# A long convolution with a gated block: transfers of 100 partitions issued as 96 and 4

## The chip, the cores and the metric

The kernel runs on one core of a Trainium2 chip. The metric is the device time of one execution in microseconds (us). TensorE (PE) multiplies matrices, VectorE (DVE), ScalarE (ACT) and GpSimd (POOL) do elementwise work, and SyncE (SP) issues transfers. ScalarE issues transfers too, in order with its own work. All transfers are moved by the core's 16 DMA engines.

## The reference

The first part is a causal convolution of `u = x * v` with a filter that a small network makes from position embeddings. The second part is a gated block on its result.

```python
h_mlp = np.maximum(pos_emb @ w1, 0.0) @ w2
h_filt = h_mlp * np.exp(-0.01 * pos)[:, None]
u = x * v                                   # (4, 12800, 128)
Uf = np.fft.rfft(u, n=2 * S, axis=1)
Hf = np.fft.rfft(h_filt, n=2 * S, axis=0)
x = x * np.fft.irfft(Uf * Hf[None], n=2 * S, axis=1)[:, :S]
# the gated block
gate_pre = sum(conv_w[k] * xp[:, k:k + S] for k in range(5))   # xp: x with 4 zero rows ahead
out = (sigmoid(gate_pre) * (x @ w_val)) @ w_out
```

Inputs and output are float32, with 4 sequences of 12800 tokens and 128 channels.

## The kernel before

The sequence of 12800 samples is cut in two blocks of 6400, and a block is seen as a grid of `N1` = 100 by `N2` = 64 samples. The transform of a block has two stages: one over the 100 samples of a column, one over the 64 of a row. Where a tile holds the first stage's side, its partitions are the 100 values of `n1` (or of `k1`, or of a row of tokens), so that tile has 100 partitions. Where it holds the second stage's side, its partitions are the 2 x 64 real and imaginary values, so it has 128. Two arrays in DRAM lie between the stages: `a_u`, the spectra after the first stage, and `c_y`, the products after the inverse's first stage.

**Phase 1** (`signal`, `filt`, `fetch`, `prep`) goes over 64 chunks: 2 blocks by 32 pairs of columns. For each chunk `fetch` (L228) has SyncE load 100 partitions of `x` and of `v`, 400 KB each, into a tile of the pool `ld`, which has six buffers. The loads are issued two chunks ahead. `prep` multiplies them on VectorE (`u_t`, L236), rounds the product on ScalarE (`u_hi`, L237) and takes the rest on GpSimd (`u_lo`, L238). Then TensorE does 12 matmuls (`fp`, L264). ScalarE and VectorE evict them into the tile `st` (L267, L269), which has three buffers. Two stores, one issued by ScalarE and one by SyncE (L272), bring 400 KB each to `a_u`. The filter's own steps are dealt out between the chunks: transposes and first matmuls (L174, L182) with eight loads of `pos` (L169), then small matmuls (`ap`, L200 and L201), then the second stage (`fk` L211 and L212, `gz` L214).

**Phase 2** goes over the 100 values of `k1`. It loads `a_u` and a table in tiles of 128 partitions (L351, L346), multiplies, forms the products on VectorE and GpSimd (L311 to L320), transforms back (L326) and stores to `c_y` from a tile of 128 partitions. All its transfers have 128 partitions.

**Phase 3** goes over 8 units (4 sequences by 2 blocks) of 8 chunks. For each chunk `prep` loads `c_y` (L438) and, for every second chunk, `x` (L431, or L434 where the two chunks do not lie together), 800 KB each of 100 partitions, into the same pool `ld`. It rounds on ScalarE (`hi`, L444) and takes the rest on VectorE or GpSimd (`lo`, L447). `conv_out` does the inverse's second stage on TensorE (`y_ps`, L412), times `x` on VectorE (L413), and transposes (L394). The gated block of one unit (`gated_out`) runs beside `conv_out` of the next, its tap sums on VectorE (L462), with output stores of 128 partitions. The first unit has no gated block beside it. The last unit is gated by rows of 100 tokens (`gated_rows`), with output stores of 100 partitions.

The order of the work on each engine is the order in which these generators are advanced in the code. Each issuing engine handles its transfers in that order, and a transfer that waits holds what is queued behind it on its engine.

Three small tables of 100 partitions (`fwd`, `win`, `inv`) are loaded once, at L129, L136 and L137.

Of the kernel before, what the change touches and what calls it, by code (L numbers as in the profile page):

```python
# [16 lines left out]

# The causal convolution of length S = 2 * M is cut in two blocks of M = N1 * N2 samples,
# n = n1 * N2 + n2. A block's polynomial is evaluated at the M roots of z^M = i,
# k = k1 + N1 * k2, in two stages (over n1, then over n2 with the twiddles in the matrix).  # L20
# With z^M = i a product of two real blocks comes back as (low half) + i (high half), so
#   y0 = Re inv(H0 U0),   y1 = Re inv(H0 U1 + (H1 - i H0) U0)
# and no block is padded.
B, S, D, FO, KC = 4, 12800, 128, 64, 5
J, N1, N2 = 2, 100, 64
M = N1 * N2
KG = 8
P1C = 2
CH = 8
# [27 lines left out]
def _narrow(nc, pool, dst, src):  # L57
    """dst (float32) = src, whose 64-bit words are doubles, rounded to nearest."""
    p, n = dst.shape
    raw = pool.tile([p, n], mybir.dt.int64, name="raw")  # L60
    nc.scalar.dma_start(out=raw, in_=src)
    words = raw.bitcast(I32).rearrange("p (n w) -> p n w", w=2)
    lo, hi = words[:, :, 0], words[:, :, 1]
    ve = nc.vector
    top = pool.tile([p, n], I32, name="top")
    tmp = pool.tile([p, n], I32, name="tmp")
    ve.tensor_scalar(out=top, in0=hi, scalar1=0x07FFFFFF, scalar2=3, op0=ALU.bitwise_and, op1=ALU.logical_shift_left)
    ve.tensor_single_scalar(out=tmp, in_=hi, scalar=-0x40000000, op=ALU.bitwise_and)
    ve.tensor_tensor(out=top, in0=top, in1=tmp, op=ALU.bitwise_or)
    ve.tensor_single_scalar(out=tmp, in_=lo, scalar=29, op=ALU.logical_shift_right)  # L70
    ve.tensor_tensor(out=top, in0=top, in1=tmp, op=ALU.bitwise_or)
    # the 29 bits below, in units of the value's own power of two
    ve.tensor_single_scalar(out=tmp, in_=lo, scalar=0x1FFFFFFF, op=ALU.bitwise_and)
    rest = pool.tile([p, n], F32, name="rest")
    ve.tensor_copy(out=rest, in_=tmp)
    ve.tensor_single_scalar(out=tmp, in_=top, scalar=-0x00800000, op=ALU.bitwise_and)
    ve.scalar_tensor_tensor(rest, rest, 2.0 ** -52, tmp.bitcast(F32), op0=ALU.mult, op1=ALU.mult)
    ve.tensor_tensor(out=rest, in0=rest, in1=top.bitcast(F32), op=ALU.add)
    # below float32's range: zero
    ve.tensor_scalar(out=tmp, in0=hi, scalar1=27, scalar2=15, op0=ALU.logical_shift_right, op1=ALU.bitwise_and)  # L80
    keep = pool.tile([p, n], F32, name="keep")
    ve.tensor_single_scalar(out=keep, in_=tmp, scalar=7, op=ALU.is_ge)
    ve.tensor_tensor(out=dst, in0=rest, in1=keep, op=ALU.mult)


@with_exitstack
def tile_longconv_gate(
# [18 lines left out]
):  # L106
    nc = tc.nc
    const = ctx.enter_context(tc.tile_pool(name="const", bufs=1))
    ld = ctx.enter_context(tc.tile_pool(name="ld", bufs=6))
    dram = ctx.enter_context(tc.tile_pool(name="dram", bufs=1, space=DRAM))  # L110

    # spectra after the first stage: [k1][re|im][n2][block][...][d]
    a_u = dram.tile([N1, 2, N2, J, B, D], F32, name="a_u")
    # products after the inverse's first stage: [block][batch][k1][re|im, n2][d]
    c_y = dram.tile([J, B, N1, 2 * N2, D], F32, name="c_y")
# [37 lines left out]

    # the filter's channels before w2, after the first stage: [re|im, n2][k1][block][channel]
    ag_pool = tc.tile_pool(name="ag", bufs=1)
    ag = ag_pool.__enter__().tile([128, N1, J, FO], F32, name="ag")

# [1 line left out]
    with tc.tile_pool(name="p1", bufs=1) as p1, tc.tile_pool(name="ps1", bufs=1, space=PSUM) as ps1:  # L159
# [4 lines left out]
        def filt():  # L164
            HC = 16
            for c0 in range(0, N2, HC):
                pos_sb = load()[:N1].rearrange("a (j n f) -> a j n f", j=J, f=FO)
                for j in range(J):
                    nc.sync.dma_start(out=pos_sb[:, j], in_=pos_v[j][:, c0:c0 + HC])  # L169
                for j in range(J):  # L170
                    for n in range(0, HC, 8):
# [17 lines left out]
                        yield  # L189
            # block 1 holds H1 - i H0  # L190
            E = 4
            for j in range(J):
                for e0 in range(0, FO, E):
# [10 lines left out]
                    yield  # L204
            # the second stage, in place: [block, channel][k1][re|im, k2]
            for k0 in range(0, N1, 4):
# [16 lines left out]
        def fetch(i):  # L223
            j, n0 = chunks[i]
            ns = slice(n0, n0 + P1C)
            t = load()[:N1].rearrange("a (w b e) -> a w b e", w=2, b=B)
            for w, src in enumerate((xv, vv)):
                nc.sync.dma_start(out=t[:, w], in_=src[j][:, :, ns].rearrange("a b n d -> a b (n d)"))  # L228
            return t[:, 0], t[:, 1]
# [15 lines left out]
        def signal():  # L245
            ready = [prep(0)]
            for i, (j, n0) in enumerate(chunks):
# [23 lines left out]
                for c in range(2):  # L271
                    (nc.scalar if c == 0 else nc.sync).dma_start(  # L272
                        out=a_u[:, c, ns, j].rearrange("k n b d -> k n (b d)"),
                        in_=st[:, c].rearrange("k n b d -> k n (b d)"))

        # the filter's steps are spread over the signal's by their time on the tensor engine
        FS = 0.9
# [13 lines left out]

# [1 line left out]
    with tc.tile_pool(name="p2", bufs=1) as p2, tc.tile_pool(name="ps2", bufs=1, space=PSUM) as ps2:  # L293
# [3 lines left out]
        def tail(k1, g_l, z_ps, h_sb):  # L297
# [7 lines left out]

            # [V0 | H0 U1 | H1' U0], then the last two added
            v_t = p2.tile([128, J + 1, BD], F32, name="v_t2", bufs=4)
# [67 lines left out]

# [1 line left out]
    with tc.tile_pool(name="p3", bufs=1) as p3, tc.tile_pool(name="ps3", bufs=1, space=PSUM) as ps3:  # L377
        xv = x.rearrange("b (j a n) d -> b j a n d", j=J, a=N1)
        HALO = KC - 1
# [3 lines left out]
        def conv_out(b, j, ext, rows=None):  # L383
            """y of one block, times x, transposed: ext[d, HALO + token]; with rows, a list
            for the chunks that are done, ext[d, HALO + n2, n1] and the last chunk first"""
            if rows is None:
# [37 lines left out]
        def prep(b, j, q):  # L424
            ns = slice(q * CH, (q + 1) * CH)
            i = order(b, j).index(q)
            if i % 2 == 0:
                x2 = load()[:N1].rearrange("k (n d) -> k n d", d=D)
                two = order(b, j)[i:i + 2]
                if two[1] == two[0] + 1:  # L430
                    nc.sync.dma_start(out=x2, in_=xv[b, j][:, q * CH:(q + 2) * CH])  # L431
                else:
                    for h, qq in enumerate(two):
                        nc.sync.dma_start(out=x2[:, h * CH:(h + 1) * CH], in_=xv[b, j][:, qq * CH:(qq + 1) * CH])  # L434
                x_now[:] = [x2]
            xt = x_now[0][:, i % 2 * CH:(i % 2 + 1) * CH]
            ct = load()[:N1, 0:2 * CH * D].rearrange("k (c e) -> k c e", c=2)
            nc.sync.dma_start(  # L438
                out=ct, in_=c_y[j, b].rearrange("k (c n) d -> k c n d", c=2)[:, :, ns].rearrange("k c n d -> k c (n d)"))
            hi = p3.tile([N1, 2, CH * D], F32R, name="hi", bufs=2)  # L440
            lo = p3.tile([N1, 2, CH * D], F32R, name="lo", bufs=2)
            for h in range(2):
                hs = slice(h * CH * D // 2, (h + 1) * CH * D // 2)
                nc.scalar.copy(out=hi[:, :, hs], in_=ct[:, :, hs])  # L444
                # until the gates run, the vector engine has room for half of this
                eng = nc.vector if h == 0 and (b * J + j) * (N2 // CH) + q < 11 else nc.gpsimd
                eng.tensor_tensor(lo[:, :, hs], ct[:, :, hs], hi[:, :, hs].bitcast(F32), op=ALU.subtract)  # L447
            return hi, lo, xt

        def gate(ext, t0, W=TCH, shift=1, pooled=0):  # L450
            """the gate's elementwise chain, an instruction at a time; pooled: taps added by GpSimd"""
            sl = lambda k: ext[:, t0 + k * shift:t0 + k * shift + W]
# [62 lines left out]
        def gated_rows(b, j, ext, rows):  # L515
            """the same by rows of N1 tokens, each chunk as soon as conv_out has it"""
            W = CH * N1
            for q in order(b, j)[1:] + order(b, j)[:1]:
# [14 lines left out]
                for g0 in range(0, CH, G):  # L533
# [4 lines left out]
                    yield  # L538
                nc.scalar.dma_start(
                    out=out[b, j * M:(j + 1) * M].rearrange("(a n) d -> a n d", a=N1)[:, q * CH:(q + 1) * CH], in_=o_sb)  # L540
# [36 lines left out]

        # the last block goes by rows, so that its gate does not wait for all of it
        b, j = units[-1]
# [49 lines left out]
```

## Time and profile before

| | |
|---|---|
| time, median of 3 runs | 1739.79 us (1730.27 to 1749.66) |
| profiled execution, span | 1744.1 us |
| TensorE / VectorE / ScalarE / GpSimd busy | 77% / 81% / 59% / 67% |
| moved by DMA | 332.97 MB, 191 GB/s in the mean |
| mean granted TensorE clock | 0.887 |

The profiled execution's span lies within the three times, so no separate share around the span can be read off. Phase 1 takes about the first 468 us, phase 2 goes on to about 1103 us, and phase 3 to the end.

A row of the table by stretches has the stretch, its length, and then the busy time and the number of instructions of TensorE, its weight loads, VectorE, ScalarE and GpSimd, followed by the granted clock, the mean busy share of the 16 DMA engines, and GB/s. A row of the chain of waits has a start, a duration and what ran. Rows of waits have who waited at which line, for whom, the total, how often, and the longest. A row of the issues has the tensors, the queue (SPq is SyncE's, ACTq is ScalarE's), the count and the size of one. A row for one line has shortest, median and longest duration in ns, and the first and last start.

### The profile page before, as it was taken

What the parts mean: (1) busy time and instruction counts of PE and PEld (TensorE: products, weight loads), DVE (VectorE), ACT (ScalarE), POOL (GpSimd) and SP (SyncE); (2) the same over time, 40 slices, a digit from 0 to 9 for tenths busy, and PEclk for the clock granted to TensorE, in tenths of its full rate; (3) what the DMA queues carried; (4) which work ended last, traced back from release to release, by engine and by line L of the source; (5) the groups of instructions that cost most, each with busy time, mean ns of one, the idle gap of its engine ahead of it and who ended that gap; (6) DMA issues with size and microseconds to landing.
All of it is one profiled execution on the core that took longest, in us unless ns stands there. A gap on an engine that the chain in (4) does not pass through costs nothing.

```text
span 1744.1 us, 16766 instructions
## 1 busy us (share of the span) xinstructions
PE 1344.8 (77%) x5313; PEld 873.4 (50%) x5313; DVE 1418.7 (81%) x1204; ACT 1032.3 (59%) x1657; POOL 1168.2 (67%) x528
## 2 busy tenths in 40 slices
PE   4679988767677777677777676588888888889896
PEld 3567766544323333233333232356766676667675
DVE  5663337653399999999999999269999999999996
ACT  2235446552477777677777775255656565556765
POOL 2223333333299988878888888159978697788752
PEclk9798997885799989998999999687988998888899
DMA  6666666666656656555656553565555455555512
GB/s 227 243 243 241 246 236 234 241 235 253 220 203 198 212 181 205 179 177 181 203 178 211 173 185 99 170 216 168 183 191 158 159 183 161 172 177 166 177 61 91
DMA packets 224831, 332.97 MB, mean 191 GB/s; under 512 B 7832, under 2 KB 162500, under 8 KB 220108
## 3 DMA queue, kind: packets, MB, share of 16 engines
q1 hardware_dynamic: 99358, 226.12, 38.8%
q10 hardware_dynamic: 125386, 105.79, 18.3%
q8 instruction: 43, 0.70, 0.2%
q14 instruction: 44, 0.36, 0.1%
HBM read 200.80 MB, written 131.07 MB: 190 GB/s over the span
## 4 chain that ended last, share of the span: by engine, by line
DVE 43%; DMA 21%; issue 15%; PE 15%; ACT 3%; POOL 2%; SPq 1%; ACTq 0%; POOLq 0%; DVEq 0%
DVE gt L462 16%; DMA a_u<-st 13%; DVE v_t L316 9%; DVE v_t L317 5%; PE fp L264 4%; DMA ld<-c_y 4%; DVE v_t L311 3%; DVE v_t L312 3%; DMA ld<-in_x_dram 3%; DVE at L413 2%; PE o_ps L506 2%; DVE gd L495 2%; PE y_ps L412 2%; PE z_ps L367 1%; PE c_ps L326 1%
## 5 line engine op out<-in xcount | busy, mean ns | idle before, releaser
L447 POOL TENSOR_TENSOR lo<-ld,hi 100x1024 fp32r<-100x1024 f32 x117 | 373.0, 3209 | 116.9 <-ACT hi L444 115.2
L462 DVE SCALAR_TENSOR_TENSOR gt<-ext,cw,gt 128x1280 f32<-128x1280 f32 (+1 forms) x164 | 411.5, 2521 | 10.2 <-POOL gt L459 5.3
L238 POOL TENSOR_TENSOR u_lo<-u_t,u_hi 100x1024 fp32r<-100x1024 f32 x64 | 154.2, 2411 | 302.3 <-ACT u_hi L237 263.5
L367 PE MATMUL z_ps<-ld 128*128 128x512 f32 x400 | 215.7, 666 | 117.3 <-DVE v_t L312 97.7
L311 POOL TENSOR_TENSOR q_t<-zsw,h_sb 128x1024 f32<-128x1024 f32 x100 | 241.6, 2416 | 90.2 <-ACT zsw L300 90.2
L316 DVE TENSOR_TENSOR v_t<-v_t,q_t 128x1536 f32<-128x1536 f32 x100 | 277.6, 2806 | 1.2 <-POOL q_t L312 1.2
L326 PE MATMUL c_ps<-v_t,ld 128*128 128x512 f32 x400 | 208.0, 639 | 57.2 <-POOL v_t L320 29.1
L312 POOL TENSOR_TENSOR q_t<-zsw,h_sb 128x512 f32<-128x512 f32 x100 | 225.8, 2258 | 0.0
L364 ACT COPY h_sb<-h_ps 64x256 f32<-64x256 f32 x400 | 147.1, 368 | 103.0 <-DVE v_t L312 66.7
L264 PE MATMUL fp<-u_hi,fwd_hi 100*100 100x512 f32 x256 | 127.6, 499 | 90.3 <-ACT st L267 59.3
L269 DVE COPY st<-fp 100x512 f32<-100x512 f32 x128 | 84.6, 687 | 127.9 <-DMA a_u<-st 100.0
L367 PEld LDWEIGHTS z_ps<-ld 128*128 128x128 f32 x400 | 76.6, 206 | 205.8 <-issue 166.9
L506 PEld LDWEIGHTS o_ps<-wout,gd 128*128 128x128 f32 x700 | 167.9, 320 | 11.9 <-issue 2.5
L317 DVE TENSOR_TENSOR v_t<-v_t 128x448 f32<-128x448 f32 x100 | 172.6, 1757 | 0.1
L444 ACT CAST hi<-ld 100x1024 fp32r<-100x1024 f32 x128 | 128.0, 1048 | 71.1 <-DMA ld<-c_y 44.5
L326 PEld LDWEIGHTS c_ps<-v_t,ld 128*128 128x128 f32 x400 | 77.9, 205 | 179.2 <-issue 123.3
L506 PE MATMUL o_ps<-wout,gd 128*128 128x128 f32 x700 | 164.2, 384 | 0.7 <-DVE gd L495 0.7
L299 ACT ACTIVATE zsw<-z_ps 64x1024 f32<-64x1024 f32 x100 | 102.2, 1022 | 61.1 <-PE z_ps L367 56.9
L311 DVE TENSOR_TENSOR v_t<-z_ps,h_sb 128x1024 f32<-128x1024 f32 x100 | 121.1, 1211 | 18.5 <-ACT zsw L300 18.5
L267 ACT COPY st<-fp 100x512 f32<-100x512 f32 x128 | 69.7, 591 | 110.7 <-DMA a_u<-st 85.6
L237 ACT CAST u_hi<-u_t 100x1024 fp32r<-100x1024 f32 x64 | 68.0, 1064 | 107.1 <-PE fp L264 51.6
L236 DVE TENSOR_TENSOR u_t<-ld 100x1024 f32<-100x1024 f32 x64 | 82.5, 1290 | 57.0 <-POOL u_lo L238 49.9
(93 smaller groups left out, 2696.8 us busy)
## 6 DMA issues: line engine op xcount, KB each, us to landing
c_y<-c_sb ACTq DMA_DIRECT2D x100, 512.0 KB
ld<-c_y SPq DMA_DIRECT2D x64, 800.0 KB
ld<-a_u SPq DMA_DIRECT2D x49, 1024.0 KB
ld<-in_x_dram SPq DMA_DIRECT2D x66, 400.0 KB
ld<-in_v_dram SPq DMA_DIRECT2D x64, 400.0 KB
a_u<-st ACTq DMA_DIRECT2D x64, 400.0 KB
a_u<-st SPq DMA_DIRECT2D x64, 400.0 KB
ld<-in_x_dram SPq DMA_DIRECT2D x31, 800.0 KB
```

What stands on the lines that cost most here:

```text
L238: nc.gpsimd.tensor_tensor(lo, u_t, hi.bitcast(F32), op=ALU.subtract)
L264: nc.tensor.matmul(out=fp, lhsT=w[:, c], rhs=d[:, b:b + 2], start=(k == 0), stop=(k == 2))
L311: eng.tensor_tensor(fl(t[:, 0:J]), fl(z), h_b(c, 0, J * B), op=ALU.mult)
L312: eng.tensor_tensor(fl(t[:, J:J + 1]), fl(z[:, 0:1]), h_b(c, 1, B), op=ALU.mult)
L316: nc.vector.tensor_tensor(v_t, v_t, q_t, op=ALU.add)
L317: nc.vector.tensor_tensor(v_t[:, 1, CUT:], v_t[:, 1, CUT:], v_t[:, 2, CUT:], op=ALU.add)
L326: nc.tensor.matmul(out=c_ps, lhsT=g_l, rhs=v_t[:, j], start=True, stop=True)
L364: nc.scalar.copy(out=h_sb[half * N2:(half + 1) * N2, c], in_=h_ps[c * N2:(c + 1) * N2])
L367: nc.tensor.matmul(out=z_ps[:, j], lhsT=f_l, rhs=au[:, j], start=True, stop=True)
L447: eng.tensor_tensor(lo[:, :, hs], ct[:, :, hs], hi[:, :, hs].bitcast(F32), op=ALU.subtract)
L462: nc.vector.scalar_tensor_tensor(gt, sl(k), cw[:, k:k + 1], gt, op0=ALU.mult, op1=ALU.add)
L506: nc.tensor.matmul(out=o_ps[:, i], lhsT=gv[:, g0 + i], rhs=wout, start=True, stop=True)
```

## The change

Every transfer of 100 partitions inside the phases is issued as two: one for partitions 0 to 95 and one for partitions 96 to 99. A small class stands in for the issuing engine and issues both, one after the other, on the same queue. The bytes, the tiles, the buffers, the queues and the order stay the same. The calls concerned are the loads of `pos`, `x` and `v` in phase 1, both stores to `a_u`, the loads of `x` and `c_y` in phase 3, and the output stores of `gated_rows`. The three tables are loaded as before. The rest of the diff removes comments.

```diff
+class _Split:
+    def __init__(self, eng):
+        self.eng = eng
+
+    def dma_start(self, out, in_):
+        for a, b in ((0, 96), (96, N1)):
+            self.eng.dma_start(out=out[a:b], in_=in_[a:b])
...
     nc = tc.nc
+    sync_s, scalar_s = _Split(nc.sync), _Split(nc.scalar)
...
-                    nc.sync.dma_start(out=pos_sb[:, j], in_=pos_v[j][:, c0:c0 + HC])
+                    sync_s.dma_start(out=pos_sb[:, j], in_=pos_v[j][:, c0:c0 + HC])
...
-                nc.sync.dma_start(out=t[:, w], in_=src[j][:, :, ns].rearrange("a b n d -> a b (n d)"))
+                sync_s.dma_start(out=t[:, w], in_=src[j][:, :, ns].rearrange("a b n d -> a b (n d)"))
...
-                    (nc.scalar if c == 0 else nc.sync).dma_start(
+                    (scalar_s if c == 0 else sync_s).dma_start(
                         out=a_u[:, c, ns, j].rearrange("k n b d -> k n (b d)"),
                         in_=st[:, c].rearrange("k n b d -> k n (b d)"))
...
-                    nc.sync.dma_start(out=x2, in_=xv[b, j][:, q * CH:(q + 2) * CH])
+                    sync_s.dma_start(out=x2, in_=xv[b, j][:, q * CH:(q + 2) * CH])
...
-                        nc.sync.dma_start(out=x2[:, h * CH:(h + 1) * CH], in_=xv[b, j][:, qq * CH:(qq + 1) * CH])
+                        sync_s.dma_start(out=x2[:, h * CH:(h + 1) * CH], in_=xv[b, j][:, qq * CH:(qq + 1) * CH])
...
-            nc.sync.dma_start(
+            sync_s.dma_start(
                 out=ct, in_=c_y[j, b].rearrange("k (c n) d -> k c n d", c=2)[:, :, ns].rearrange("k c n d -> k c (n d)"))
...
-                nc.scalar.dma_start(
+                scalar_s.dma_start(
                     out=out[b, j * M:(j + 1) * M].rearrange("(a n) d -> a n d", a=N1)[:, q * CH:(q + 1) * CH], in_=o_sb)
```

## The prediction

> **What bounds the kernel now.** I read the page first, then the busy time of each engine by stretches, then the chain of waits inside the first phase, SyncE's queue beside it, and the list of waits.
>
> ```profile
> span 1744.1 us, 16766 instructions
> PE 1344.8 (77%) x5313; PEld 873.4 (50%) x5313; DVE 1418.7 (81%) x1204; ACT 1032.3 (59%) x1657; POOL 1168.2 (67%) x528
> DMA  6666666666656656555656553565555455555512
> ```
>
> Over the whole span VectorE looks like the bound, at 81%. But the DMA digits stand at 6 through the first eleven slices and never reach 7. The table by stretches shows what that means (PE, PEld, DVE, ACT, POOL busy, clock, DMA share, GB/s):
>
> ```profile
> 0.00:30.00 30.00, 13.31 (x40) 9.01 (x40) 14.30 (x26) 7.74 (x14) 7.26 (x7) 1.00 0.65 217
> 30.00:110.00 80.00, 53.64 (x267) 40.94 (x268) 52.72 (x84) 20.72 (x31) 23.89 (x10) 0.83 0.67 244
> 110.00:190.00 80.00, 75.99 (x587) 58.76 (x585) 33.78 (x50) 39.18 (x54) 26.71 (x11) 0.91 0.67 242
> 190.00:270.00 80.00, 74.32 (x511) 54.96 (x507) 32.16 (x42) 36.80 (x57) 29.08 (x12) 0.94 0.67 240
> 270.00:350.00 80.00, 60.21 (x268) 45.37 (x266) 54.48 (x100) 50.14 (x114) 26.31 (x12) 0.83 0.67 238
> 350.00:430.00 80.00, 57.46 (x191) 38.40 (x192) 36.99 (x56) 33.19 (x62) 28.48 (x12) 0.73 0.68 244
> 430.00:468.00 38.00, 24.08 (x78) 15.12 (x77) 14.95 (x17) 12.86 (x19) 12.69 (x5) 0.72 0.57 192
> 602.50:605.00 2.50, 2.50 (x8) 1.32 (x7) 2.50 (x2) 1.91 (x2) 2.50 (x2) 1.00 0.96 377
> 630.50:635.50 5.00, 4.63 (x13) 2.09 (x11) 5.00 (x2) 4.88 (x10) 4.66 (x2) 1.00 0.97 360
> 1121.00:1165.00 44.00, 34.80 (x150) 22.71 (x149) 18.25 (x22) 21.26 (x30) 17.02 (x8) 0.85 0.62 222
> 1165.00:1187.00 22.00, 18.64 (x68) 12.09 (x67) 22.00 (x16) 13.20 (x20) 21.56 (x7) 0.68 0.59 187
> 1187.00:1650.00 463.00, 398.33 (x1784) 319.48 (x1784) 444.77 (x318) 277.88 (x378) 383.42 (x129) 0.89 0.54 173
> ```
>
> From 30 to 430 us the DMA share is 0.67 or 0.68 in every row, whatever the compute engines do. In phase 2, where all transfers have 128 partitions, short stretches reach 0.96 and 0.97, at 360 to 377 GB/s. So 0.67 is a ceiling of the phase 1 transfers, which have 100 partitions. 0.67 of 16 engines is 10.7. The largest number of engines up to 16 over which 100 rows can be dealt evenly is 10 (128 rows: 16). I read it so: ten engines work without a pause, six stand idle.
>
> The chain of waits and SyncE's queue agree:
>
> ```profile
> 206.05 11.86 DMA a_u<-st
> 219.75 12.22 DMA a_u<-st
> 233.37 12.84 DMA a_u<-st
> ```
>
> ```profile
> 206.05 3.28 SPq L272 DMA_DIRECT2D a_u<-st  x1
> 209.43 0.81 SPq L228 DMA_DIRECT2D ld<-in_x_dram  x1
> 210.30 2.48 SPq L228 DMA_DIRECT2D ld<-in_v_dram  x1
> 212.87 3.30 SPq L272 DMA_DIRECT2D a_u<-st  x1
> ```
>
> ```profile
> DVE st L269 <- DMA a_u<-st: 100.0, 32, 6.2
> ACT st L267 <- DMA a_u<-st: 85.6, 30, 9.5
> SPq L228 <- DMA fwd<-in_tab_fwd_dram: 1.8, 1, 1.8
> ACT hi L444 <- DMA ld<-c_y: 44.5, 13, 12.0
> ```
>
> Nearly the whole chain from 191 to 262 us is stores of `st`: each takes 12 us to land, and the evictions that want its buffer wait (100.0 and 85.6 us). SyncE goes from one issue to the next without a rest, at 2.5 to 3.3 us each: it is held back by full queues. One chunk takes 212.87 - 206.05 = 6.82 us.
>
> From 1187 us on VectorE is 444.77 of 463 us busy: there DMA does not decide. Between them lies phase 3's first block (1103 to 1187 us): VectorE is free (18.25 of 44 us), the share again 0.62, and ScalarE waits for `c_y` (44.5 us).
>
> **The change part by part.** Transfers that become two, by the list of issues:
>
> ```profile
> ld<-c_y SPq DMA_DIRECT2D x64, 800.0 KB
> ld<-in_x_dram SPq DMA_DIRECT2D x66, 400.0 KB
> ld<-in_v_dram SPq DMA_DIRECT2D x64, 400.0 KB
> a_u<-st ACTq DMA_DIRECT2D x64, 400.0 KB
> a_u<-st SPq DMA_DIRECT2D x64, 400.0 KB
> ld<-in_x_dram SPq DMA_DIRECT2D x31, 800.0 KB
> ld<-in_pos_emb_dram SPq DMA_DIRECT2D x8, 400.0 KB
> out_dram<-o_sb ACTq DMA_DIRECT2D x8, 400.0 KB
> c_y<-c_sb ACTq DMA_DIRECT2D x100, 512.0 KB
> ```
>
> The last row, of 128 partitions, stays whole. The others add 64+66+64+64+64+31+8+8 = 369 issues: 297 on SyncE, 72 on ScalarE. The three table loads of 100 partitions stay as they are.
>
> *The rate.* 96 rows deal evenly over 16 engines, six each; the other 4 rows give at best one more to four of them. The busiest engine then moves 7 rows of 100 in place of 10: a factor of 0.70, or 242 / 0.70 = 346 GB/s, below the 360 that phase 2 reaches. The trace has no transfer of 96 or of 4 rows, so this has bounds: 0.63 (100/16 rows, and four engines not felt) to 1.00 (all 4 rows on one engine, 6+4 = 10). I take 0.70, because 128 rows, the nearest row of the kind, do fill 16 engines.
>
> [...]
>
> *Phase 1's loop.* With DMA at 0.70, 80 us become at least 56 and the last 38 become 27. The next bound is TensorE. Its busy column (76.0 and 74.3 of 80 us from 110 to 270) counts modelled ends and stretches at half clock and is an upper bound; weight loads, one per matmul, give the lower one (58.8 and 55.0). I take the middle, 67 and 65. The other stretches have nothing above 60.2 (VectorE at most 54.5, ScalarE 50.1). Floors: 56 + 67 + 65 + 56 + 56 + 27 = 327 us for 438. All engines then stand near their limits together, in queues kept in program order, so I add 9%, an estimate: VectorE as the bound runs at 96% (444.77/463) where one engine decides, and here three do. That makes 357 us, 5.6 us a chunk: gain 81 us. Bounds: 438 - 327 = 111 at best, with the lower TensorE bound 438 - (56+59+56+56+56+27) = 128; at worst below nothing (the rivals).
>
> *Phase 1's head* (30 us): the same kind of transfers at 0.65, but more issues ahead of the tables on which ScalarE waits. I put it at nothing, give or take 5.
>
> *Phase 2*: all its transfers have 128 partitions. Nothing changes.
>
> *Phase 3's first block*: 84 us, held by DMA for the first 62 (1103 to 1165) and by both for 22. At 0.70 the 62 would lose 19; TensorE's 34.80 of 44 us leave at most 9 in the row that is shown, so some 13 of 62. In the 22 VectorE is busy throughout, so I count 2. Gain 15; bounds 5 to 25. After 1187 us VectorE is the bound: nothing.
>
> *The issues themselves.* Held back by nothing, one issue takes:
>
> ```profile
> L272 ACTq DMA_DIRECT2D a_u<-st x64: 281/282/333, 29.8 to 459.1; - x64
> L438 SPq DMA_DIRECT2D ld<-c_y x64: 750/757/897, 1102.7 to 1643.6; - x64
> 1099.39 3.21 DMA c_y<-c_sb
> ```
>
> SyncE issues three transfers per chunk of phase 1, then six: 6 x 0.28 = 1.7 us of 5.6, hidden by the wait for room. ScalarE gets 64 x 0.28 = 18 us more in phase 1, where its busiest stretch is 50.14 of 80. In phase 3, 64 x 0.76 more on SyncE lie ahead of loads two chunks early. A second wait at each reader is hidden with them; uncovered, all 72 on ScalarE would cost 20 us.
>
> *What gets scarcer.* SyncE's fifth load starts only here:
>
> ```profile
> 4.82 0.80 SPq L228 DMA_DIRECT2D ld<-in_x_dram  x1
> ```
>
> It waited for the landing of `fwd`, an unrelated table and the first DMA of the program (1.8 us, in the waits above). Ahead of it stand four loads of SyncE and, in the order of the code and at the same pace, four of ScalarE. I read it as eight completion counters dealt out in turn. A phase 1 chunk has four transfers, so the counters span two chunks; with eight they span one. A transfer must then have landed before its successor one chunk later is issued, with the rest of SyncE's queue, or of ScalarE's evictions, behind it. Landing is 12 us now, but mostly queueing: two chunks are 3.28 MB, 13.5 us at 242 GB/s. One chunk is 1.64 MB, 4.7 us at 346 GB/s. The fixed part, from the 3.21 us of a 512 KB store that has the engines to itself, is 3.21 - 0.524/0.36 = 1.75 us. While one transfer's end is reported, the others keep the engines busy, so I count this within the 9%.
>
> Sum: 1744 - 81 - 15 = 1648 us. The three times, 1730 to 1750 with median 1740, straddle the span, so I take the page's own time as typical.
>
> **The rivals.** *The counters cost the fixed part every time*: a chunk takes 4.7 + 1.75 = 6.5 us against 6.82. Over 63 periods that is 20 us, and 1744 - 20 - 15 = 1709. For it: SyncE issues in order. Against: four transfers in flight cover one another. Chance 0.12.
>
> *Slower*: landing shrinks only with the rate and not with the backlog, 11.86 x 0.70 = 8.3 us; with one chunk per round of counters the period is 8.3, (8.3 - 6.82) x 63 = 93 us more, 1744 + 93 - 15 = 1822. It decides as soon as a landing takes more than 6.8 us. Against it: half the bytes can be waiting. Chance 0.06.
>
> *It does not do what it says*: the pieces do not spread, one engine still moves 10 rows, and the time stays near 1744. For it: no row of this trace has 96 or 4. Against: 128 rows do spread. Chance 0.07.
>
> [...]
>
> **How the numbers follow.** The forecast has 0.75: its own range is 1744 - 128 - 25 = 1591 to about 1690 (loop gain 45, phase 3's 9). The range for 8 in 10 leaves out the bottom of that, where no engine loses anything, and takes in the first rival: 1605 to 1712. Three runs of before spread by 1.1%, so about 1% can be told from no change. Faster by over 1% holds the forecast and most of the first rival, 0.86; within 1%, the third and a rest of the first, 0.08; slower 0.06.
>
> **What would show it.** DMA share above 0.67 in the first slices, toward 0.8 to 0.95, at 290 GB/s or more; phase 1 ending near 387 us in place of 468; waits of L269 and L267 for `a_u<-st` well below 100.0 and 85.6 us; the `a_u<-st` landings at 4 to 6 us; phase 2 as long as before, and VectorE still over 95% busy after the first block. Wrong, if the share stays at 0.67 (no spread), or rises while SyncE's issues wait for landings of older loads (counters), or if TensorE is full from 110 to 270 us and the gain is lost there.

## The result and the profile after

The changed kernel takes 1665.82 us (median, 1663.25 to 1668.40), and the kernel before, beside it on the same chip, 1744.72 us (1730.27 to 1751.33). The ratio is 0.9557, with a 95% interval of 0.9499 to 0.9615. The forecast was 1648 us, with a range of 1605 to 1712. The direction is right and the time lies within the range, but the gain is 79 us where 96 were forecast, and a part of those 79 has a cause that the prediction did not have.

The page of the changed kernel, its span, busy times and DMA digits:

```profile
span 1665.5 us, 17379 instructions
PE 1312.5 (79%) x5313; PEld 855.8 (51%) x5313; DVE 1403.6 (84%) x1204; ACT 1029.6 (62%) x1657; POOL 1184.0 (71%) x528
DMA  9998899997666555665556555786676666676413
```

The first nine slices, which were all 6, are now 8 and 9: by this share, engines that stood idle now work. In phase 2 the line looks as it did, and in phase 3 its digits rise from 5 to 6 and 7.

To see where the 78.6 us between the two spans (1744.1 and 1665.5) come from, I cut both at three points: the first load of `a_u` (phase 1 over), the first product `at` (phase 3 has begun) and the first tap sum `gt` (its first block is over). Each row has the first start behind the three durations. First the kernel before, then the changed one:

```profile
L351 SPq DMA_DIRECT2D ld<-a_u x51: 343/360/484, 468.3 to 1031.2; - x51
L413 DVE TENSOR_TENSOR at<-y_ps,ld x128: 673/678/693, 1118.7 to 1684.5; 100x512 f32<-100x512 f32 x128
L462 DVE SCALAR_TENSOR_TENSOR gt<-ext,cw,gt x164: 1037/2466/6090, 1168.2 to 1733.2; 128x1280 f32<-128x1280 f32 x140, 128x800 f32<-128x800 f32 x24
```

```profile
L363 SPq DMA_DIRECT2D ld<-a_u x51: 344/360/476, 408.0 to 970.9; - x51
L425 DVE TENSOR_TENSOR at<-y_ps,ld x128: 672/678/693, 1060.8 to 1609.7; 100x512 f32<-100x512 f32 x128
L474 DVE SCALAR_TENSOR_TENSOR gt<-ext,cw,gt x164: 1037/2450/6039, 1104.1 to 1654.3; 128x1280 f32<-128x1280 f32 x140, 128x800 f32<-128x800 f32 x24
```

| stage | before | after | gain |
|---|---|---|---|
| phase 1 | 468.3 | 408.0 | 60.3 |
| phase 2, to the first `at` | 650.4 | 652.8 | -2.4 |
| phase 3, first block | 49.5 | 43.3 | 6.2 |
| phase 3, the rest (to the span's end) | 575.9 | 561.4 | 14.5 |

Each column is one execution. A second profile of the changed kernel, from another chip, ends phase 1 at 414.8 us, with 651.6, 42.0 and 563.1 us for the other stages. So some 7 us of phase 1 and 2 of the others can't be told from scatter. Of the kernel before there is one profile, and its executions spread over 21 us, so the gains of single stages rest on the other runs below as well.

The table by stretches of the changed kernel, with the same columns as before:

```profile
30.00:110.00 80.00, 61.16 (x297) 44.52 (x296) 59.10 (x97) 24.12 (x35) 28.90 (x12) 0.89 1.00 297
110.00:190.00 80.00, 78.06 (x657) 62.79 (x656) 30.86 (x36) 40.38 (x54) 26.71 (x11) 0.91 0.87 247
190.00:270.00 80.00, 75.92 (x486) 55.37 (x484) 45.18 (x64) 48.57 (x84) 34.26 (x14) 0.96 0.91 270
270.00:350.00 80.00, 65.65 (x308) 48.43 (x307) 63.57 (x113) 55.77 (x125) 37.64 (x14) 0.89 0.97 292
350.00:400.00 50.00, 38.85 (x139) 24.45 (x140) 27.30 (x32) 22.57 (x35) 27.14 (x11) 0.90 0.90 278
1061.00:1101.00 40.00, 32.98 (x157) 23.62 (x156) 20.62 (x24) 20.86 (x31) 19.77 (x8) 0.84 0.96 220
1123.00:1575.00 452.00, 401.10 (x1826) 324.41 (x1825) 430.34 (x326) 282.52 (x387) 396.49 (x131) 0.91 0.65 178
```

The share is 1.00 from 30 to 110 us and 0.97 from 270 to 350, so the transfers do spread over all 16 engines and still decide there. But full engines move 297 and 292 GB/s, not 346. From 110 to 270 us TensorE is busy 78.06 and 75.92 of 80, and the share falls: there it seems to have taken over. The chain of waits agrees. From 190 to 270 us its steps on TensorE make up about 69% and its transfers 21%, where before the stores of `st` alone made up 92%. From 110 to 190 us the difference is small, 62% on TensorE against 55% before. In phase 3's first block (the row from 1061 us), where only loads run, the share rises from 0.62 to 0.96 but the rate stays, at 220 GB/s against 222. In the last row, after the first block, VectorE is busy 95% of the time, as the prediction said.

The waits of the changed kernel, first those of the engines, then those of SyncE's queue (its line is that of the helper):

```profile
ACT st L279 <- DMA a_u<-st: 7.3, 3, 3.9
DVE st L281 <- DMA a_u<-st: 5.0, 2, 3.3
ACT hi L456 <- DMA ld<-c_y: 29.6, 5, 17.1
...
SPq L94 <- DMA ld<-in_x_dram: 52.3, 50, 2.6
SPq L94 <- DMA ld<-in_v_dram: 45.8, 46, 3.9
SPq L94 <- DMA a_u<-st: 35.6, 50, 1.7
```

The evictions hardly wait for stores any more (85.6 and 100.0 us before). SyncE now does wait for older transfers to land, 134 us in all, though never longer than 3.9 us at a time.

Two places of the chain of waits: stores in phase 1, and phase 2's last store.

```profile
71.93 4.73 DMA a_u<-st
76.74 6.24 DMA a_u<-st
83.06 4.69 DMA a_u<-st
...
1037.99 13.20 DMA c_y<-c_sb
```

A store of `st` lands after 5 to 6 us in place of 12. But phase 2's last store, a transfer that the change doesn't touch, takes 13.20 us where it took 3.21. The head of phase 3 has become slower.

### The profile page after: what moved, and what is told of

Read it like the earlier page. It is cut to its first block, busy times and chain, and to the rows that moved or that the text cites. A ratio compares the mean times of both kernels' runs of the same rounds, so it can differ in the third digit from the quotient of the medians.

```text
span 1665.5 us, 17379 instructions
## 1 busy us (share of the span) xinstructions
PE 1312.5 (79%) x5313; PEld 855.8 (51%) x5313; DVE 1403.6 (84%) x1204; ACT 1029.6 (62%) x1657; POOL 1184.0 (71%) x528
## 4 chain that ended last, share of the span: by engine, by line
DVE 41%; PE 23%; DMA 16%; issue 16%; ACT 2%; POOL 2%; ACTq 0%; SPq 0%; DVEq 0%; POOLq 0%
DVE gt L474 13%; DVE v_t L328 10%; DMA a_u<-st 6%; DVE v_t L329 5%; PE fp L276 5%; PE y_ps L424 4%; DMA ld<-in_v_dram 4%; DVE v_t L323 3%; DVE v_t L324 3%; PE o_ps L518 3%; DVE at L425 2%; PE z_ps L379 2%; DMA ld<-c_y 2%; DVE gd L507 2%; PE c_ps L338 2%
## 5 line engine op out<-in xcount | busy, mean ns | idle before, releaser
L459 POOL TENSOR_TENSOR lo<-ld,hi 100x1024 fp32r<-100x1024 f32 x117 | 379.4, 3269 | 90.3 <-ACT hi L456 86.0
L474 DVE SCALAR_TENSOR_TENSOR gt<-ext,cw,gt 128x1280 f32<-128x1280 f32 (+1 forms) x164 | 386.1, 2369 | 7.4 <-POOL gt L471 7.0
L250 POOL TENSOR_TENSOR u_lo<-u_t,u_hi 100x1024 fp32r<-100x1024 f32 x64 | 163.5, 2559 | 235.4 <-ACT u_hi L249 214.6
L379 PE MATMUL z_ps<-ld 128*128 128x512 f32 x400 | 219.1, 675 | 117.0 <-DVE v_t L324 97.2
L276 PE MATMUL fp<-u_hi,fwd_hi 100*100 100x512 f32 x256 | 117.6, 459 | 53.4 <-ACT u_hi L249 23.7
L248 DVE TENSOR_TENSOR u_t<-ld 100x1024 f32<-100x1024 f32 x64 | 88.5, 1384 | 51.1 <-POOL u_lo L250 34.1
L408 ACT COPY ext<-tp 128x400 f32<-128x400 f32 x128 | 68.4, 542 | 84.3 <-PE tp L406 83.7
L339 ACT COPY c_sb<-c_ps 128x512 f32<-128x512 f32 x200 | 110.8, 588 | 14.2 <-PE c_ps L338 10.7
```

Of the source, the lines that this page charges most:

```text
L250: nc.gpsimd.tensor_tensor(lo, u_t, hi.bitcast(F32), op=ALU.subtract)
L276: nc.tensor.matmul(out=fp, lhsT=w[:, c], rhs=d[:, b:b + 2], start=(k == 0), stop=(k == 2))
L379: nc.tensor.matmul(out=z_ps[:, j], lhsT=f_l, rhs=au[:, j], start=True, stop=True)
L474: nc.vector.scalar_tensor_tensor(gt, sl(k), cw[:, k:k + 1], gt, op0=ALU.mult, op1=ALU.add)
```

## The experiments

All have the kernel before run beside them on their own chip. Below, phase 1 ends at the first load of `a_u`, and "the rest of phase 3" is the span from the first `gt` on.

**Only phase 1's transfers cut.** The four calls of phase 3 go back to whole transfers.

```diff
-            sync_s.dma_start(
+            nc.sync.dma_start(
                 out=ct, in_=c_y[j, b]...   # the same for both loads of x, and for the store of gated_rows
```

> Only the transfers of phase 1 are split. Theory: the gain comes from the rate of each stage's own transfers, so phase 1 ends near 408 us as in the changed kernel (468 before) and phase 3 takes as long as before (about 641 us from its first load of c_y): 1745 - 60 = about 1685 us. Rival: phase 3's later units became shorter (448 to 434 us between the same two chunks) because VectorE and GpSimd happen to meet differently after a changed start, whatever the loads do; then phase 3 shortens here too and the time is 1665 to 1672 us.

Measured: 1665.63 us, ratio 0.9546 (0.9515 to 0.9576). That is the changed kernel's time, and the rival's, so the cuts in phase 3 earn nothing in sum that shows. Its three first starts:

```profile
L363 SPq DMA_DIRECT2D ld<-a_u x51: 344/360/480, 409.8 to 972.8; - x51
L425 DVE TENSOR_TENSOR at<-y_ps,ld x128: 673/678/693, 1057.9 to 1613.0; 100x512 f32<-100x512 f32 x128
L474 DVE SCALAR_TENSOR_TENSOR gt<-ext,cw,gt x164: 1035/2452/6036, 1107.3 to 1655.1; 128x1280 f32<-128x1280 f32 x140, 128x800 f32<-128x800 f32 x24
```

Its first block takes 49.4 us, as before. Yet the rest of phase 3 takes 1665.1 - 1107.3 = 557.8 us, in place of 575.9, although its code is now that of the kernel before.

**Only phase 3's transfers cut.** The three calls of phase 1 go back.

```diff
-                sync_s.dma_start(out=t[:, w], in_=src[j]...)
+                nc.sync.dma_start(out=t[:, w], in_=src[j]...)   # the same for pos and for both stores to a_u
```

> Only the transfers of phase 3 are split. Theory: phase 1 as before (468 us), phase 3 as in the changed kernel, so 1745 - 20 = about 1725 us, with the early 96-row loads of c_y again in the way of phase 2's last stores (first rounding some 17 us after the last of these is issued, 12 before). Rival (a shift of VectorE against GpSimd and not the loads): about 1740 us or more.

Measured: 1728.36 us, ratio 0.9899 (0.9868 to 0.9929). Phase 1 ends at 474.4 us, 6 us later than before, which is no more than the two profiles of the changed kernel differ by. The first block takes 43.5 us, 6 less than before, and the rest of phase 3 takes 558.2 us, as in the run above. So the first block's 6 us belong to phase 3's cuts. The 15 us after it come with either half of the change.

**Twice the transfers, all of 100 partitions.** Each transfer is cut in two by columns.

```diff
-        for a, b in ((0, 96), (96, N1)):
-            self.eng.dma_start(out=out[a:b], in_=in_[a:b])
+        h = out.shape[1] // 2
+        for a, b in ((0, h), (h, 2 * h)):
+            self.eng.dma_start(out=out[:, a:b], in_=in_[:, a:b])
```

> Every transfer that the change splits is split in the free dimension in place of the partitions: two transfers of 100 partitions and half the columns. The number of transfers, and with it the number of issues and of completion counters per chunk, is that of the changed kernel; the rows stay on as many engines as before. Theory (the gain is the spread over more engines, the counters cost next to nothing): phase 1 as before, 468 us give or take 8, and 1735 to 1755 us in all. Rival (the counters cost the fixed part of a landing): a chunk takes 1.64 MB / 242 GB/s + 1.75 us = 8.5 us in place of 6.8, phase 1 is up to 107 us longer, and the time is 1780 to 1850 us. Rival (the gain came from smaller pieces): as fast as the changed kernel, 1666 us.

Measured: 1727.64 us, ratio 0.9900 (0.9875 to 0.9924). The stretch that DMA holds, the first load of `a_u`, and two stores of the chain:

```profile
30.00:110.00 80.00, 54.49 (x248) 39.48 (x246) 47.82 (x84) 19.56 (x29) 23.34 (x10) 0.83 0.67 245
```

```profile
L364 SPq DMA_DIRECT2D ld<-a_u x51: 348/360/605, 468.4 to 1032.1; - x51
```

```profile
34.15 6.76 DMA a_u<-st
...
216.37 6.99 DMA a_u<-st
```

With eight transfers per chunk phase 1 ends at 468.4 us, as before. The number of transfers costs nothing that shows, and cutting alone gives nothing there: share and rate stay at 0.67 and 245 GB/s. The 1% comes after phase 1: 3 us up to the first `at`, 5 in the first block, and 10 in the rest of phase 3 (565.7 us). A store of half the size now lands in 7 us, not 12, at the same rate. Its 200 KB fewer are 0.8 us at 245 GB/s, so by this estimate most of the landing time was backlog.

**Pure movement.** A kernel that leaves out the whole computation and, in one stretch after the other, moves 12 transfers with rows of 8 KB. Each stretch changes one thing: the number of rows, the partition that they start at, or their distance in DRAM.

```python
def load_64_at0(i):
    nc.sync.dma_start(out=big[0:64, i], in_=rows_of(i, 64, 1))
def load_64_at32(i):
    nc.sync.dma_start(out=big[32:96, i], in_=rows_of(i, 64, 1))
def load_96_4_step(i):                      # rows 64 KB apart in DRAM
    s = rows_of(i, 100, 8)
    nc.sync.dma_start(out=big[0:96, i], in_=s[0:96])
    nc.sync.dma_start(out=big[96:100, i], in_=s[96:100])
```

> Leaves out the whole computation and only moves data: seventeen stretches of twelve transfers each, rows of 8 KB. What is asked: why the changed kernel moves 297 GB/s in phase 1 and 220 GB/s in phase 3's first block with all engines busy (share 1.00 and 0.96), where loads of 128 partitions in phase 2 reach 360. [...] Theory D (DRAM: rows that lie 64 KB apart are slow): with rows that lie together 96 and 64 rows anywhere go at over 320 GB/s, and stepped rows at 250 or less with 128 partitions too. [...]

The stretches (start and end, length, busy VectorE and GpSimd, clock, DMA share, GB/s). Loads: 64 rows from partition 0, 64 from partition 32, then rows 64 KB apart: 128, 96, 100, and 96+4. Stores: 128, 100, 96+4.

```profile
255.00:283.00 28.00, 0.00 (x0) 0.00 (x0) 1.00 1.01 206
288.00:303.00 15.00, 0.00 (x0) 0.00 (x0) 1.00 1.01 397
349.00:377.00 28.00, 0.00 (x0) 0.00 (x0) 1.00 1.01 424
381.00:418.00 37.00, 0.00 (x0) 0.00 (x0) 1.00 1.01 248
422.00:470.00 48.00, 0.00 (x0) 0.00 (x0) 1.00 0.57 203
475.00:518.00 43.00, 0.00 (x0) 0.00 (x0) 1.00 0.97 217
572.00:601.00 29.00, 0.00 (x0) 0.00 (x0) 1.00 1.01 420
605.00:646.00 41.00, 0.00 (x0) 0.00 (x0) 1.00 0.61 229
650.00:686.00 36.00, 0.00 (x0) 0.00 (x0) 1.00 0.85 263
```

The same 64 rows move at 206 GB/s from partition 0 and at 397 from partition 32, with all engines busy in both. So the rate depends on which partitions are touched, not only on how many engines work. 96 rows from partition 0 fill the engines (1.01) and move at 248 GB/s (246 from partition 32), where 128 rows reach 424. The distance in DRAM is not the cause, since 128 rows have it too. Loads alone gain little from 96+4 (203 to 217), stores alone somewhat more (229 to 263).

Why 96 rows fall to 248 isn't settled here. The runs show rates by partition; the paths into the on-chip memory that the rivals of two later runs name were not shown.

**Pure movement, other cuts, both directions at once.** The whole computation is left out here too; SyncE loads and ScalarE stores together.

```python
CUTS = {"100": ((0, 100),), "96_4": ((0, 96), (96, 100)), "36_64": ((0, 36), (36, 100)), "128": ((0, 128),), ...}
def load(i, cuts):
    for a, b in cuts:
        nc.sync.dma_start(out=big[a:b, i], in_=s[a:b])
def store(i, cuts):
    for a, b in cuts:
        nc.scalar.dma_start(out=orow[i * 128 + a:i * 128 + b], in_=one[a:b, i % 6])
```

> Leaves out the whole computation and only moves data: twenty stretches of twelve transfers of rows of 8 KB. Asked: what the pieces of four rows cost, and whether other cuts of 100 rows are faster. [...] Stores of 64 rows at 0 against 32 show whether reading the on-chip memory has the same limit: half the rate, or the same.

Both directions with 100, 96+4, 36+64 and 128 rows:

```profile
565.00:642.00 77.00, 0.00 (x0) 0.00 (x0) 1.00 0.62 252
647.00:702.00 55.00, 0.00 (x0) 0.00 (x0) 1.00 0.98 348
767.00:820.00 53.00, 0.00 (x0) 0.00 (x0) 1.00 0.94 362
890.00:947.00 57.00, 0.00 (x0) 0.00 (x0) 1.00 1.01 418
```

With both directions at once 96+4 gains what the prediction counted: 252 / 348 = 0.72. So the factor of 0.70 is about right for mixed traffic in rows of 8 KB, and the cut 0 to 35 and 36 to 99 is better still, at 362. Stores alone agree (262 GB/s with 96+4, 277 with 36+64). Loads alone do not: 96+4 moves 232 GB/s, 36+64 only 219 and 80+20 only 212, so other cuts gain nothing there. Pieces of 4 rows alone move 30 GB/s in loads and 25 in stores, at a share of 0.28 and 0.25. Stores of 64 rows go at 205 GB/s from partition 0 and 416 from partition 32, the same difference that loads have (206 and 397).

**Phase 1, loads alone cut.** As the first run, and both stores to `a_u` whole.

```diff
-                    (scalar_s if c == 0 else sync_s).dma_start(
+                    (nc.scalar if c == 0 else nc.sync).dma_start(
                         out=a_u[:, c, ns, j]...
```

> Only the loads of phase 1 (pos, x, v) are split, its stores are whole again, and phase 3 is whole. Theory (seven rows in place of ten on the busiest engine, for loads and stores alike): 17 rows in place of 20 for a load and a store, a factor of 0.85, phase 1 near 435 us, and with the 18 us of phase 3 that every variant has had: about 1694 us. Rival (paths into the on-chip memory, on which 96+4 rows load at 212 GB/s and 100 rows at 196 in the kernel that only moves data): 0.96, phase 1 near 455 us, 1714 us.

Measured: 1690.49 us, ratio 0.9667 (0.9628 to 0.9707).

**Phase 1, stores alone cut.** As the first run, and the loads of `pos`, `x` and `v` whole.

```diff
-                sync_s.dma_start(out=t[:, w], in_=src[j]...)
+                nc.sync.dma_start(out=t[:, w], in_=src[j]...)   # the same for pos
```

> Only the stores of phase 1 (a_u) are split, its loads are whole again, and phase 3 is whole. Theory (rows on the busiest engine): as for the loads, phase 1 near 435 us, about 1694 us. Rival (paths; stores of 96+4 rows went at 257 GB/s and of 100 at 222): 0.93, phase 1 near 440 us, 1699 us. If the stores' landing as such decides, since the evictions wait for it, this one brings most of the 60 us and the loads little.

Measured: 1696.04 us, ratio 0.9699 (0.9654 to 0.9744). First the run with loads cut, then two first starts of the run with stores cut:

```profile
L363 SPq DMA_DIRECT2D ld<-a_u x51: 349/360/572, 435.1 to 996.5; - x51
```

```profile
L363 SPq DMA_DIRECT2D ld<-a_u x51: 344/360/506, 420.0 to 987.6; - x51
L474 DVE SCALAR_TENSOR_TENSOR gt<-ext,cw,gt x164: 1037/2313/6094, 1121.1 to 1685.0; 128x1280 f32<-128x1280 f32 x140, 128x800 f32<-128x800 f32 x24
```

The loads alone win 33 us of phase 1, the stores alone 48, both together 58.5 in the run that cuts phase 1 only. For the loads the theory had the end of phase 1 right (435). For the stores both theory (435) and rival (440) were 15 us and more too late, and that the time came out between their 1694 and 1699 us is luck, as phase 3 shows below. The gains don't add up. A likely reason is TensorE, which from 110 to 190 us is busy 78.06 of 80 us with both cut and 75.99 before, so the other half finds less to win there.

The second run shows something else. Its phase 1 is 15 us shorter than that of the run with loads cut, but it ends later: the rest of its phase 3 takes 1695.0 - 1121.1 = 573.9 us, as in the kernel before. The order of GpSimd's instructions in phase 3, `l` for a step of `lo` (L459) and `V` for one of the gated block's `vl`, by their start:

```
before        llllllllllVVlllVllllVllllVllllllVVllVllllVllllVllllVllVll
stores alone  llllllllllVVlllVllllVllllVllllllVVllVllllVllllVllllVllVll
changed       llllllllllVVlllVllllllVllVllllVllVllllVllVllllVllllVVllll
phase 1 only  llllllllllVVlllVllllllVllVllllVllVllllVllVllllVllllVVllll
```

The code of phase 3 is the same in the first, second and fourth of them. The program is built with `schedule_with_timeline_sim=True`, at the kernel's last lines: a planner sets the instructions in an order of its own, and another list of transfers in phase 1 gives another order on the engines in phase 3. So what is said of the kernel above, that the order is that in which the generators are advanced, holds only as far as the planner keeps to it. The stores-alone run has the order of before on VectorE, ScalarE, GpSimd and TensorE in phase 3, and phase 3's old length. The run with twice the transfers has a third order on GpSimd and 565.7 us. All other runs of the whole kernel have GpSimd's new order, and from the first `gt` on they take 558 to 563 us.

The order differs in phase 1 too. TensorE's in the changed kernel parts from that of before after 8 matmuls, and in the run with twice the transfers after 16. As that run ends phase 1 at 468.4 us, another order alone did not bring phase 1's gain.

The group of VectorE's tap sums (busy, mean ns of one, idle before), of the kernel before, the changed one, and the one with stores alone:

```profile
L462 DVE SCALAR_TENSOR_TENSOR gt<-ext,cw,gt 128x1280 f32<-128x1280 f32 x140 | 381.8, 2740 | 4.5 <-ACT gt L455 4.5
```

```profile
L474 DVE SCALAR_TENSOR_TENSOR gt<-ext,cw,gt 128x1280 f32<-128x1280 f32 x140 | 358.8, 2578 | 0.2
```

```profile
L474 DVE SCALAR_TENSOR_TENSOR gt<-ext,cw,gt 128x1280 f32<-128x1280 f32 x140 | 380.0, 2727 | 4.5 <-ACT gt L467 4.5
```

The same 140 instructions take 23 us less in the new order, on the engine that bounds phase 3. The order and the length go together in every run: a tap sum takes 2740 and 2727 ns in the mean in the two runs with the old order, 2652 in the third order, and 2567 to 2589 in the nine profiles with the new one. But no run changes the order alone.

**The first `c_y` loads whole.** Asked whether phase 3's head can be mended.

```diff
-            sync_s.dma_start(
+            (nc.sync if b == j == 0 and q < 4 else sync_s).dma_start(
                 out=ct, in_=c_y[j, b]...
```

> As the changed kernel, but the first four loads of c_y stay whole, so that all of them wait for phase 2's last store. Theory (the early 96-row loads queue ahead of phase 2's last stores, whose landing goes from 3 to 13 us, and the pieces of 4 rows then wait for these): the last store lands in 3 to 4 us again, the first rounding starts some 12 us after it is issued (17 in the changed kernel), and the time falls by 4 to 6 us, to about 1661. Rival (the early start wins as much as it costs): 1666 give or take 2.

Measured: 1674.51 us, ratio 0.9624 (0.9573 to 0.9675), slower than the changed kernel by 9 us. The last store lands in 3.25 us again, as expected. But the first block grows to 54.3 us, in place of 43.3 and 42.0 in the two profiles of the changed kernel. From the first load of `a_u` to the first `gt` it takes 701.8 us, the changed kernel 696.1 and 693.6. So my theory that undoing the early start gains time fell. The edit takes from these four loads both the early start and the spread over 16 engines, so it doesn't say which of the two was worth more than the late store costs.

**Another cut: 36 and 64 rows.**

```diff
-        for a, b in ((0, 96), (96, N1)):
+        for a, b in ((0, 36), (36, N1)):
```

> As the changed kernel, but cut into partitions 0 to 35 and 36 to 99. The busiest engine again moves 7 rows (3 + 4), and no piece has 4 rows. In the kernel that only moves data this cut went at 348 GB/s in both directions at once, 96+4 at 334. Theory (phase 1's stretches at a DMA share of 0.97 to 1.00 are held by that rate): they get about 4% shorter, phase 1 ends near 400 us in place of 408, and fewer rows of c_y are loaded early, so phase 3's head gains some 3 us more: 1655 to 1660 us. Rival (rows of 1 KB and the queues set the rate here): phase 1 at 408 give or take 3, 1662 to 1668 us.

Measured: 1649.81 us, ratio 0.9477 (0.9427 to 0.9527). The first load of `a_u`, the stretch that DMA held, and phase 2's last store in the chain:

```profile
L363 SPq DMA_DIRECT2D ld<-a_u x51: 358/360/567, 398.8 to 964.5; - x51
```

```profile
30.00:110.00 80.00, 65.28 (x347) 48.76 (x346) 57.12 (x96) 28.01 (x40) 31.19 (x13) 0.89 0.94 299
```

```profile
1030.48 5.42 DMA c_y<-c_sb
```

Phase 1 ends 9 us earlier than in the changed kernel, as expected, but not by the expected way. In the stretch that DMA held the rate is 299 GB/s where the changed kernel has 297 (291 and 293 in the second profiles of both, from the runs on one chip below), and not 4% more. The gain shows from 110 to 270 us, at 267 and 274 GB/s against 247 and 270, where TensorE is as good as full in both (80.00 and 79.01 of 80 us, against 78.06 and 75.92). There the planner has set another order again, which parts from the changed kernel's after 52 matmuls. So the cut's own part in the 9 us isn't separated from the order's. The other 8 lie ahead of the first `gt`: 4.6 up to the first `at`, with the last store landing after 5.42 us in place of 13.20, and 3.5 in the first block. The rest of phase 3 is about as long (560.3 against 561.4 us).

**The filter's matmuls spread more evenly.** If TensorE is the bound from 110 to 270 us, its load there could be moved. The weights by which the filter's steps are dealt out are raised for `ap`.

```diff
-        cost = [0.7, 0.9] * (J * N2 // 8) + [0.8] * (FO // 4) + [1.6] * (FO // 4) + [0.9] * (N1 // 4)
+        cost = [0.7, 0.9] * (J * N2 // 8) + [1.1] * (FO // 4) + [2.2] * (FO // 4) + [0.9] * (N1 // 4)
```

> As the changed kernel, but the planned cost of the filter's small matmuls (ap) is 1.1 and 2.2 in place of 0.8 and 1.6, so that they are dealt over more chunks and the other filter steps over fewer. Theory (TensorE, 78 and 76 of 80 us busy, holds the changed kernel from 110 to 270 us, where the DMA share falls to 0.87 and 0.91, while DMA holds the rest): TensorE's busiest stretch falls below 75 of 80, and phase 1 ends 5 to 12 us earlier, 1655 to 1661 us. Rival (TensorE's busy time there is mostly modelled ends): phase 1 at 408 give or take 3, 1663 to 1669 us.

Measured: 1667.61 us, ratio 0.9574 (0.9511 to 0.9636): no gain.

```profile
110.00:190.00 80.00, 79.17 (x661) 61.61 (x660) 32.40 (x37) 42.49 (x56) 27.49 (x12) 1.00 0.89 253
```

TensorE is as full as it was (79.17 of 80), so the edit didn't take the load away. Whether a real relief would gain anything stays open.

**The changed kernel and the cut at 36 on one chip.** No edit; the two were to be compared side by side.

> The changed kernel once more, beside the cut into 36 and 64 partitions on the same chip. Theory (the cut into 36 and 64 is faster by itself, 9 us in phase 1 and 9 us in phase 3's head): 1663 to 1669 us here, and 14 to 20 us less there. Rival (another chip made the difference): the two within 6 us of each other.

> The cut into 36 and 64 partitions once more, on the same chip as the changed kernel. Theory: 1647 to 1652 us, phase 1 at 399 us and the first block of phase 3 as before. Rival: within 6 us of the changed kernel beside it.

Measured: 1667.49 us for the changed kernel (0.9563, 0.9499 to 0.9627) and 1647.65 us for the cut at 36 (0.9461, 0.9408 to 0.9514). In their profiles phase 1 ends at 414.8 and 400.0 us. So it was not the chip: the second is 20 us faster than the changed kernel beside it and the fastest version of this study.

## Why the prediction was right or wrong

- **What bounds phase 1** was right. The ceiling of 0.67 was idle engines, and 96 rows filled them (1.00). The prediction read 0.67 as ten of 16 engines. Ten would be 0.625; moved alone, 100 rows show 0.57 to 0.62, and why the kernel's 0.67 lies above that stays open. Moved alone, 96 and 128 rows show 1.01, and 4 rows 0.28 and 0.25, which agrees with rows dealt evenly. The same share with twice the transfers (0.67) shows that the rows per transfer did it, not the cutting.
- **The rate's factor of 0.70** was mis-sized, and this is the term by which phase 1's gain fell short. It took the busiest engine's rows as the whole cost, with full engines at 346 GB/s. Measured is 297 GB/s, 242 / 297 = 0.815. The runs with movement alone show why engines that are all busy need not be fast: the rate depends on which partitions they touch (64 rows at 206 GB/s from partition 0 and 397 from 32, at a share of 1.01 in both). What in the kernel keeps it at 297, where 8 KB rows reach 348 in both directions, wasn't tested.
- **The sum over phase 1** with that one term put right: 65 + 67 + 65 + 65 + 65 + 31 = 358 us of floors in place of 327. Measured from 30 to 408 us is 378 (385 in the second profile). So the allowance for several bounds at once is 20 to 27 us, near the 30 counted. The 31 us of the floors, less what the allowance had too much, are the 21 us by which phase 1's gain of 60 fell short of 81.
- **TensorE as the next bound** agrees with its busy time from 110 to 270 us (78.06 and 75.92 of 80) and with the chain of waits, though no run lightened it. What held was the fall of the evictions' waits (85.6 and 100.0 us to 7.3 and 5.0) and of the landings (12 to 5 or 6 us).
- **Phase 3's first block, 15 us**: the step failed. It gained 6.2 us, and the head ahead of it lost 2.4; against the run with whole transfers in phase 3 the two together are 1.4 us (697.5 to 696.1). The prediction took the factor of 0.70 for these loads too (62 us less 19). The share did rise, from 0.62 to 0.96, but not the rate (222 and 220 GB/s; 222 in the run that cuts phase 3 alone), as loads alone gain little in pure movement too (203 to 217). So the 6.2 us don't come from a faster rate. That they come from the early start of the first loads is likely and not separated; that these loads would start early, into phase 2's last stores, the prediction did not see.
- **"After 1187 us VectorE is the bound: nothing"**: the bound was right, the nothing wrong. 14.5 us came from there, and they go with another order of the instructions, under which VectorE's own tap sums are 23 us shorter. That the time of phase 3 came near the forecast (18.3 us against 15) is a coincidence.
- **The counters rival and the slower rival** did not come true. Eight transfers per chunk left phase 1 at 468.4 us, where the fixed part on top of each chunk's 6.8 us would have cost 63 x 1.75 = 110, and landing time shrank with the backlog (12 us to 5 or 6), which was the prediction's argument against the slower one. The sign that it named for them did appear, SyncE waiting for older loads, but with 2.6 and 3.9 us at most, beside engines that were full. In the run with twice the transfers such waits add up to 223 us, none over 3.8, and phase 1 is as long as before. That the counters are eight stays my reading of one wait (1.8 us, for `fwd`).
- **"It does not do what it says"** did not come true: the share rose to 1.00 and the time fell by 4.4%.

## What to carry to other kernels

A DMA share that stands still at a fraction of 1, whatever the engines do, can point to the number of rows per transfer (0.67 with 100 rows here, 1.00 with 96 and 4). Once the engines are full, look at GB/s and try other cuts, since two with the same 7 rows on the busiest engine, by my count, differ by 20 us here. Don't size such a gain by the count of engines alone: with rows of 8 KB in both directions it came out (0.72 for 0.70), in phase 1 it didn't (0.815), and for the loads of phase 3's first block nothing came of it. When a stage gains whose work wasn't touched, compare the instruction order of both traces before looking for a cause on the chip; a variant that keeps the old order is the control. The same check is due where two cuts are compared.

## What was not expected of the hardware

- 64 partitions moved at 206 GB/s from partition 0 and 397 from partition 32, at the same share of 1.01. So a share of 1 was not a full rate.
- A load that starts early can hold up a store: the first cut `c_y` loads of phase 3 start at 1028.4 us, ahead of phase 2's last store at 1038.0, since 96 of their rows need only earlier stores. That store then lands after 13.20 us in place of 3.21, and after 3.25 in the run that leaves these loads whole. ScalarE's issue of it took 6136 ns, against 366 as a rule. The transfers of `c_y` from 1020 to 1062 us (ns shortest, median, longest; first and last start):

```profile
L94 SPq DMA_DIRECT2D ld<-c_y x8: 546/604/697, 1028.4 to 1053.3; - x8
L340 ACTq DMA_DIRECT2D c_y<-c_sb x5: 366/367/6136, 1025.0 to 1038.0; - x5
```

- One and the same VectorE instruction, a tap sum of 128x1280, takes from 1534 to 6090 ns in the kernel before, and its mean follows the order that it shares with GpSimd's work: 2740 ns in one, 2578 in another. In the trace of before, the 8 of the 140 beside which GpSimd did nothing took 1536 to 1540 ns, and each of the 107 that took over 1600 ns overlaps an instruction of GpSimd. That the two engines get in each other's way is how I read it; no run takes GpSimd's work away.
